# Quarter products, in-place sums and PSUM hand-over in a fused attention and SiLU kernel

## The chip, the cores and the metric

The kernel runs on one core of one Trainium2 chip. The metric is the device time of one execution in microseconds; the median of the runs is compared. All data is float32, and all work of the five engines (TensorE, VectorE, ScalarE, GpSimd, SyncE) is ordered by semaphores. In the profile they are PE (matmul) and PEld (its weight loads), DVE, ACT, POOL and SP.

## The reference, cut to what matters

```python
# q, k, v: (8, 12, 448, 64); w_in: (768, 2048); w_out: (2048, 768)
q_n, k_n = rmsnorm(q, g_q), rmsnorm(k, g_k)
attn = softmax(q_n @ k_n.T / sqrt(64))            # for each batch and head
x = (attn @ v).transpose(0, 2, 1, 3).reshape(3584, 768)
h = x @ w_in
return (h / (1 + exp(-h))) @ w_out                # (3584, 768)
```

## The kernel before

**Stages.** First comes the attention, 24 steps of four heads each (`visit`, `between`), with the product by w_in of batches that are done already mixed in between. When the last step is visited, the product by w_in of the last two batches is left; it runs alone (`halves_in` with `prepare_out` beside it). Its activated result, the 2048 features of all 3584 rows, lies in DRAM as `hidden`. The last stage is the product by w_out: seven quads of 512 rows (`quad`, L1079), each fetched from `hidden` in four pieces of 1 MB, two halves of the rows by two halves of the features.

**Seven products for eight.** Both products use the same scheme. A product of two matrices cut in 2 x 2 blocks needs eight block products; Winograd's form needs seven, and additions before and after. With a for the left side and b for the right:

```
s1 = a21 + a22   s2 = s1 - a11    s3 = a11 - a21   s4 = a12 - s2
t1 = b12 - b11   t2 = b22 - t1    t3 = b22 - b12   t4 = b21 - t2
p1 = a11 b11   p2 = a12 b21   p3 = s4 b22   p4 = a22 t4   p5 = s1 t1   p6 = s2 t2   p7 = s3 t3
u2 = p1 + p6   c11 = p1 + p2   c12 = u2 + p5 + p3
u3 = u2 + p7   c21 = u3 + p4   c22 = u3 + p5
```

The quad's left side is 512 rows by 2048 features, the right is w_out, 2048 by 768. One such product of halves is 256 rows by 1024 features by 384 columns. It can be done as one (`single`, once for each of the two tiles of 128 rows: eight multiplications with 384 columns), or by the same scheme a second time (`deep`: seven products of quarters, each of four multiplications with 192 columns). In quads 1 to 6, products 4, 7, 3 and 2 are done by seven and 1, 5 and 6 as one. In quad 0 all are done as one; beside them VectorE computes the sums of the right quarters (`sums_deep_right`) that later quads use.

**Where data lies.** The four pieces of a quad are `left[i, r]`. The quad's sums s1, s2 and s4 share one further buffer, `left_sum`; s3 overwrites a21. Sums of quarters of the features go to two alternating buffers `deep_lefts`, sums of the right quarters to `deep_rights`. All of these come by `take` from `regions`, memory of earlier stages. `stage` is one of them: it also holds the rows on their way to `hidden`.

**Who does what.** TensorE writes PSUM. ScalarE copies some products out of PSUM, VectorE adds the others to what they are added to (`plus`, L703) and makes the sums (`minus`, L700). Additions that touch no PSUM go to GpSimd where the code says `add_pool` (L1077). SyncE issues the fetches (`fetch`, L973) and the stores of results (`store`, L451), in the order of the program.

**The order.** Nothing is scheduled by a planner: within an engine, instructions run in the order in which the Python code issues them (`manual_schedule`). In `quad` the order of products is 1, 5, 4, 6, 7, 3, 2.

**PSUM.** It has eight banks. Up to the end of the w_in stage one pool, `ps`, holds them all: two `mm`, two `sc` of two banks each, `av0` and `av1`. While the w_in stage runs alone, `bank` (L725) takes these six tiles in turn, which leaves one bank of each `sc` unused. Then `banks.close()` gives the pool back, and `ps_out` opens with two banks `one` for whole products and six `seventh` for quarters. `Seven` is the w_in stage's form of the scheme; its additions `five` partly run on GpSimd.

Of the kernel before, what the change touches and what calls it, by code (L numbers as in the profile page):

```python
# [13 lines left out]
ALU = mybir.AluOpType  # L14
# [442 lines left out]
def bounded(  # L457
# [7 lines left out]
    banks = ctx.enter_context(ExitStack())  # L465
    ps = banks.enter_context(tc.tile_pool(name="ps", bufs=1, space=bass.MemoryType.PSUM))
# [255 lines left out]
    alone = False  # L722
    order = ["mm", "mm", "sc", "sc", "av0", "av1"]

    def bank(n):  # L725
        if not alone:
            return ps.tile([P, BANK], F32, name="mm", bufs=2)[:, 0:n]
        name = order[0]
        order.append(order.pop(0))
        if name == "sc":  # L730
            return ps.tile([P, 2, BANK], F32, name=name, bufs=2)[:, 0, 0:n]
        if name == "mm":
            return ps.tile([P, BANK], F32, name=name, bufs=2)[:, 0:n]
        return ps.tile([P, BANK], F32, name=name)[:, 0:n]
# [185 lines left out]
    def prepare_out(m):  # L920

        if m == HF // 2:
            for at in ((0, 0), (1, 0), (1, 1)):
                fetch(0, *at)
        for _ in range(room.CHUNK):
            rounder.open()
            yield
            rounder.round()
        if m % 2:
            right_sums(*chunk_out(ORDER[m // 2]))  # L930
        yield
# [8 lines left out]
        work, sets[1], sums_x, room.chunk(3), room.sums(3), stage, ring, parts  # L940
    ]
    regions = [[a, 0] for a in regions]

    def take(n, *which):

        for i in which:
            a, at = regions[i]
            if at + n <= a.shape[1]:
                regions[i][1] += n
                return a[:, ds(at, n)]  # L950
        raise AssertionError

    size = HF * 2 * P
    left = {(0, 0): take(size, 0), (1, 0): take(size, 0), (1, 1): take(size, 0)}
    left[0, 1] = take(size, 1)
    left_sum = take(size, 2)
    deep_lefts = [take(3 * size // 4, 3) for _ in range(2)]
    DEEP = (4, 7, 3, 2)
    deep_rights = {
        name: take(3 * 4 * QUARTER, *at).rearrange("p (s i k) -> p s i k", s=3, i=4)  # L960
        for name, at in zip(DEEP, ([4], [6], [1], [5]))
    }
    results = {at: take(2 * z.HALF, i) for at, i in (((1, 1), 0), ((2, 2), 0), ((2, 1), 6), ((1, 2), 6))}
    aside = [take(2 * z.HALF, 2) for _ in range(2)]
    copies = [[take(QUARTER, 1, 7) for _ in range(4)] for _ in range(2)]

    def fetch(q, i, r):
# [6 lines left out]

    LEFTS = {
        1: left[0, 0], 2: left[0, 1], 3: left_sum, 4: left[1, 1],
        5: left_sum, 6: left_sum, 7: left[1, 0],
    }

    def sums_left(*which):  # L980

        a11, a12, a21, a22, x = (
            a.rearrange("p (n c) -> p n c", n=2)
            for a in (left[0, 0], left[0, 1], left[1, 0], left[1, 1], left_sum)
        )
        for n in range(2):
            left_sums(
                *(a[:, n] for a in (a11, a12, a21, a22)), x[:, n], x[:, n], x[:, n], which
            )
# [5 lines left out]
    def deep_left(name):  # L995

        a = LEFTS[name].rearrange("p (i m t c) -> p m t i c", i=4, m=2, t=2)
        s = deep_lefts[DEEP.index(name) % 2].rearrange("p (s i c) -> p s i c", s=3, i=4)
        return a[:, 0, 0], a[:, 1, 0], a[:, 0, 1], a[:, 1, 1], s[:, 0], s[:, 1], s[:, 2]

    def deep_right(name, i):
        b = right_one(name, i)
        s = deep_rights[name]
        h = [ts(k, QUARTER) for k in range(2)]
        return b[:, 0, h[0]], b[:, 0, h[1]], b[:, 1, h[0]], b[:, 1, h[1]], s[:, 0, i], s[:, 1, i], s[:, 2, i]

    def sums_deep_right(name, last):

        for i in ORDER:
            b11, b12, b21, b22, t1, t2, t4 = deep_right(name, i)  # L1010
            if last:
                minus(b22, b12, b12)
            else:
                minus(b12, b11, t1)
                minus(b22, t1, t2)
                minus(b21, t2, t4)

    def of_seven(name, a, b):

        a11, a12, a21, a22, s1, s2, s4 = a  # L1020
# [3 lines left out]
            5: (s1, t1), 6: (s2, t2), 7: (a21, b12),  # L1024
        }[name]

    def deep(name, out, then=lambda t, h: None):

        a = deep_left(name)
        out = out.rearrange("p (t h k) -> p t h k", t=2, h=2)  # L1030
        p1, u2, u3, p5 = copies[DEEP.index(name) % 2]

        def product(of):
            t = ps_out.tile([P, BANK], F32, name="seventh", bufs=6)[:, 0:QUARTER]
# [4 lines left out]

        nc.scalar.copy(p1, product(1))  # L1040
        plus(product(2), p1, out[:, 0, 0])
        then(0, 0)
        plus(product(6), p1, u2)
        nc.scalar.copy(p5, product(5))
        plus(product(7), u2, u3)
        add_pool(u2, p5, u2)
        add_pool(u3, p5, out[:, 1, 1])
        plus(product(4), u3, out[:, 1, 0])
        then(1, 1)
        then(1, 0)  # L1050
        plus(product(3), u2, out[:, 0, 1])
        then(0, 1)

    def single(name, t):

        a = LEFTS[name].rearrange("p (f t c) -> p f t c", f=HF, t=2)
        o = ps_out.tile([P, BANK], F32, name="one", bufs=2)[:, 0 : z.HALF]
# [8 lines left out]
    def save_out(q, i, j, t):  # L1066
        store(
            nc, out, z, (4 * q + 2 * (i - 1) + t) * P, results[i, j][:, ts(t, z.HALF)],
            (j - 1) * z.HALF,
        )  # L1070

    def both(f):
        for t in range(2):
            f(t)

    def add_pool(a, b, o):
        nc.gpsimd.tensor_tensor(out=o, in0=a, in1=b, op=ALU.add)  # L1077

    def quad(q):  # L1079
        c = results  # L1080
        half = lambda a, t: a[:, ts(t, z.HALF)]
        which = DEEP if q > 0 else ()

        def spread(t=None):

            x, c12, c22, c21 = (
                a if t is None else half(a, t) for a in (aside[0], c[1, 2], c[2, 2], c[2, 1])
            )
            add_pool(c12, c22, c12)
            add_pool(c22, x, c22)  # L1090
            add_pool(c21, x, c21)
            for k in range(2) if t is None else (t,):
                save_out(q, 2, 2, k)
                save_out(q, 2, 1, k)

        p1 = [single(1, 0), single(1, 1)]
        fetch(q, 0, 1)
        sums_left(0, 2)
        both(lambda t: nc.scalar.copy(half(c[1, 1], t), p1[t]))
        if q == 0:  # L1100
            sums_deep_right(4, False)
        both(lambda t: nc.scalar.copy(half(c[2, 2], t), single(5, t)))
        if 4 in which:
            left_sums(*deep_left(4))
        sums_left(1)
        fetch(q + 1, 0, 0)
        if 4 in which:
            left_sums(*deep_left(7))
            deep(4, c[2, 1])
        else:  # L1110
            both(lambda t: nc.scalar.copy(half(c[2, 1], t), single(4, t)))
            sums_deep_right(7, False)
            sums_deep_right(4, True)
        fetch(q + 1, 1, 1)
        for t in range(2):
            plus(single(6, t), half(c[1, 1], t), half(c[1, 2], t))
        sums_left(3)
        if 7 in which:
            left_sums(*deep_left(3))
            deep(7, aside[0])  # L1120
            plus(aside[0], c[1, 2], aside[0])
            spread()
        else:
            for t in range(2):
                plus(single(7, t), half(c[1, 2], t), half(aside[0], t))
                spread(t)
            sums_deep_right(3, False)
            sums_deep_right(7, True)
        fetch(q + 1, 1, 0)
        if 2 in which:  # L1130
            left_sums(*deep_left(2))
        if 3 in which:
            deep(3, aside[1])
            add_pool(c[1, 2], aside[1], c[1, 2])
            both(lambda t: save_out(q, 1, 2, t))
        else:
            for t in range(2):
                plus(single(3, t), half(c[1, 2], t), half(c[1, 2], t))
                save_out(q, 1, 2, t)
            sums_deep_right(2, False)  # L1140
            sums_deep_right(3, True)
        if q == QUADS - 1:

            def last(t, h):
                columns = ds((2 * t + h) * QUARTER, QUARTER)
                rows = c[1, 1][:, columns]
                plus(rows, aside[0][:, columns], rows)
                store(
                    nc, out, z, (4 * q + t) * P, rows, h * QUARTER,
                    *((nc.scalar, nc.sync)[:: 1 if h else -1]),  # L1150
                )

            deep(2, aside[0], last)
        elif 2 in which:
            deep(2, aside[0])
            add_pool(c[1, 1], aside[0], c[1, 1])
            both(lambda t: save_out(q, 1, 1, t))
        else:
            for t in range(2):
                plus(single(2, t), half(c[1, 1], t), half(c[1, 1], t))  # L1160
                save_out(q, 1, 1, t)
        if q == 0:
# [400 lines left out]
```

## Time and profile before

| | us |
|---|---|
| median of 3 runs | 1401.07 (1399.28 to 1401.15) |
| the profiled execution | 1397.43 |
| its span in the trace | 1395.6 |
| PE busy | 1352.6 (97%) |
| DVE busy | 799.7 (57%) |
| ACT busy | 509.0 (36%) |
| POOL busy | 433.7 (31%) |
| last attention product ends, w_in alone begins | 781.0 |
| product by w_out begins | 911.3 |
| its last multiplication ends | 1389.7 |

A time in the trace is counted from the start of the span. An engine's busy time is an average over stages that have different limits; what a change in one stage is worth is read from the chain of waits in that stage. A multiplication of float32 leaves two records in the trace, so that counts of PE there are twice the number of multiplications. Tiles are named by the memory that they lie in: `work`, `x`, `sums_x`, `W`, `rows`, `stage` and `parts` in the w_out stage are the regions from which `take` cut the buffers.

### The profile page before, as it was taken

To read this page: it belongs to the slowest core of one execution; us is meant where nothing else is said; L and a number is where in the kernel's file an instruction comes from. 1 tells how busy PE (TensorE), PEld (TensorE's weight loads), DVE (VectorE), ACT (ScalarE), POOL (GpSimd) and SP (SyncE) were. 2 spreads that over 40 slices of the span, in tenths; PEclk is the share of its full clock that TensorE was granted. 3 is DMA by queue.
4 is the path that set the end of the run, shared out by engine and by line. 5 is a ranking of instruction groups with operands and counts; after the bars stand their busy time and mean duration, and the time that the engine had idled before them with its cause. 6 is when DMAs were issued, how large, how long until landed. Compare 5 with 4: busy or idle time off the path is not lost.

```text
span 1395.6 us, 18420 instructions
## 1 busy us (share of the span) xinstructions
PE 1352.6 (97%) x6849; PEld 775.0 (56%) x6849; DVE 799.7 (57%) x1157; ACT 509.0 (36%) x852; POOL 433.7 (31%) x316
## 2 busy tenths in 40 slices
PE   7998999999999999999999999989999999999998
PEld 4333444444444444444444455555687879696967
DVE  3887876765644444644444686654554545454635
ACT  6876555645455455445544254310000000000000
POOL 4664442433233333332320244401031313130403
PEclk9999999999999999999999999999999999999999
DMA  7654335333223223223211367323213232323211
GB/s 186 182 150 132 114 107 153 82 91 80 78 75 96 79 75 101 77 74 94 75 50 54 105 202 255 121 86 95 72 54 116 78 113 67 102 65 102 65 42 48
DMA packets 175686, 139.32 MB, mean 100 GB/s; under 512 B 104036, under 2 KB 159716, under 8 KB 175588
## 3 DMA queue, kind: packets, MB, share of 16 engines
q1 hardware_dynamic: 175264, 137.86, 33.2%
q8 instruction: 56, 0.92, 0.3%
q14 instruction: 42, 0.34, 0.1%
q10 hardware_dynamic: 324, 0.20, 0.0%
HBM read 88.47 MB, written 41.29 MB: 93 GB/s over the span
## 4 chain that ended last, share of the span: by engine, by line
PE 87%; DVE 6%; ACT 2%; issue 2%; DMA 1%; SPq 1%; POOL 0%; DVEq 0%; ACTq 0%; POOLq 0%
PE mm L749 26%; PE one L1060 19%; PE seventh L1037 16%; PE av L610 9%; PE sc L578 8%; PE av L749 3%; PE sc L749 3%; DVE work L653 2%; PE sc L545 1%; PE sc L560 1%; PE mm L644 1%; PE sc L644 1%; DVE rms L396 1%; DVE work L624 1%; ACT work L583 1%
## 5 line engine op out<-in xcount | busy, mean ns | idle before, releaser
L749 PE MATMUL mm<-x,W 128*128 128x448 f32 x654 | 261.0, 543 | 10.6 <-DVE stage L703 7.4
L424 POOL TENSOR_TENSOR rms<-rms,minus_half 128x14 f32<-128x14 f32 (+4 forms) x55 | 138.5, 2520 | 248.7 <-DVE rms L420 190.3
L583 ACT ACTIVATE work<-sc,rms 128x448 f32<-128x448 f32 x324 | 184.1, 631 | 86.3 <-PE sc L578 75.9
L749 PEld LDWEIGHTS mm<-x,W 128*128 128x128 f32 x654 | 121.0, 190 | 137.3 <-issue 107.8
L749 PE MATMUL mm<-sums_x,W 128*128 128x448 f32 x474 | 190.5, 542 | 2.3 <-DVE stage L703 1.5
L578 PE MATMUL sc<-work 64*64 64x448 f32 x1344 | 164.2, 546 | 5.5 <-ACT work L583 3.7
L624 DVE TENSOR_TENSOR work<-work 128x896 f32<-128x896 f32 (+1 forms) x114 | 123.3, 1115 | 76.3 <-ACT work L583 75.5
L610 PE MATMUL av<-work,rows 64*64 64x448 f32 x1296 | 153.1, 546 | 7.7 <-issue 2.9
L749 PEld LDWEIGHTS mm<-sums_x,W 128*128 128x128 f32 x474 | 88.6, 190 | 91.7 <-issue 83.0
L1060 PE MATMUL one<-W,sums_x 128*128 128x384 f32 x360 | 121.0, 486 | 0.0
L610 PEld LDWEIGHTS av<-work,rows 64*64 64x64 f32 x1296 | 51.8, 133 | 95.8 <-issue 86.1
L578 PEld LDWEIGHTS sc<-work 64*64 64x64 f32 x1344 | 51.8, 133 | 87.2 <-issue 35.4
L1060 PEld LDWEIGHTS one<-W,sums_x 128*128 128x128 f32 x360 | 68.4, 190 | 47.7
L764 POOL TENSOR_TENSOR parts<-parts,stage 128x448 f32<-128x448 f32 x31 | 42.4, 1368 | 168.3 <-DVE parts L703 168.2
L396 DVE TENSOR_REDUCE rms<-squares 112x8 f32<-112x512 f32 (+1 forms) x80 | 52.4, 655 | 63.0 <-ACT squares L395 62.1
L1060 PE MATMUL one<-W,work 128*128 128x384 f32 x216 | 72.6, 486 | 0.0
L882 ACT ACTIVATE stage<-stage 128x896 f32<-128x896 f32 x63 | 57.2, 945 | 26.2 <-DVE stage L703 25.6
L395 ACT ACTIVATE squares<-rows 128x512 f32<-128x512 f32 (+1 forms) x74 | 44.8, 605 | 57.8 <-DVE rms L396 56.7
L1040 ACT COPY x<-seventh 128x192 f32<-128x192 f32 x24 | 7.6, 318 | 156.6 <-PE seventh L1037 151.2
L1077 POOL TENSOR_TENSOR x<-x 128x192 f32<-128x192 f32 x12 | 7.1, 591 | 177.0 <-DVE x L703 177.0
L653 DVE RECIPROCAL work<-sc 128x224 f32<-128x224 f32 x36 | 55.7, 1548 | 11.1 <-PE sc L644 11.1
L700 DVE TENSOR_TENSOR sums_x<-sums_x,work 128x1024 f32<-128x1024 f32 x14 | 17.2, 1226 | 72.1 <-PE one L1060 71.7
(194 smaller groups left out, 1996.6 us busy)
## 6 DMA issues: line engine op xcount, KB each, us to landing
hidden<-stage SPq DMA_DIRECT2D x63, 448.0 KB, 2.8
work<-hidden SPq DMA_DIRECT2D x21, 1024.0 KB, 4.9
rows<-in_moe_w_out_dram SPq DMA_DIRECT2D x32, 384.0 KB, 3.2
W<-in_moe_w_in_dram SPq DMA_DIRECT2D x22, 512.0 KB, 4.6
rows<-in_k_dram SPq DMA_DIRECT2D x48, 192.0 KB, 3.0
work<-work SPq DMA_DIRECT2D x144, 56.0 KB, 1.9
rows<-in_q_dram SPq DMA_DIRECT2D x36, 224.0 KB, 3.5
x<-hidden SPq DMA_DIRECT2D x7, 1024.0 KB, 5.6
```

The source lines that it names most:

```text
L395: nc.scalar.activation(t, rows, AF.Square)
L396: nc.vector.tensor_reduce(out=out, in_=t.rearrange("p (n d) -> p n d", n=n), axis=AX.X, op=ALU.add)
L424: nc.gpsimd.tensor_tensor(out=t, in0=t, in1=half, op=ALU.pow)
L578: nc.tensor.matmul(two[ds(half * D, D), h, 0:S], keys[rows, ts(half, D)], qT[rows, pair, :], start=True, stop=True,)
L583: nc.scalar.activation(eleft[:, h] if j == LEFT else weights(c, j)[:, i, h], two[:, h, 0:S], AF.Exp, scale=norm.column(c, i, h, j),)
L610: nc.tensor.matmul(sums[i][ds(h * D, D), :], v, w, start=(j == 0 and step == 1), stop=(j == LEFT - 1 and step == 1),)
L624: nc.vector.tensor_tensor(out=total, in0=total, in1=more, op=ALU.add)
L653: nc.vector.reciprocal(out=r[0][:, rows], in_=t[:, rows])
L749: nc.tensor.matmul(t, self.left(name, s), self.right(name, s), start=s == ends[0], stop=s == ends[1])
L882: nc.scalar.activation(t, t, AF.Silu)
L1037: nc.tensor.matmul(t, x[:, i], y, start=i == ORDER[0], stop=i == ORDER[-1])
L1060: nc.tensor.matmul(o, a[:, 2 * i + m, t], right_one(name, i)[:, m], start=n == 0, stop=n == len(steps) - 1,)
```

## The change

It changes the w_out stage and the use of PSUM.

- Six of the seven products are done by seven in quads 1 to 6: 4, 2, 5, 6, 7 and 3; product 1 remains as one. In quad 0, products 7 and 3 are done by seven too. The order of products is 4, 1, 2, 5, 6, 7, 3.
- `left_sum` is gone: s1 overwrites a22, s2 overwrites a11, s4 overwrites a12 and s3 overwrites a21, as before. In the products of quarters s3 has a place of its own, and the quarters of the features are left as they are.
- Products 2, 6 and 3 are added to results that are there already (`more`), block by block, and p1 is copied twice. All additions of the stage are on VectorE, none on GpSimd. One set of `copies` takes the place of two. There are 18 buffers of right sums instead of 12 (in four larger ones).
- Of quad 0, the pieces a22, a11 and a12 are fetched during the w_in stage, a21 at the start of the quad; before, a12 was the late one.
- A pool `ps_mm` of two banks stays open for the whole kernel. The other six banks are given back when the attention is done (`others.close()`), and a pool `ps_alone` of six takes them. While the w_in stage runs alone, `bank` takes one of `ps_mm` at every fourth turn and one of `ps_alone` otherwise. In the w_out stage whole products use `ps_mm`, quarters `ps_alone`.

```diff
     def bank(n):
-        if not alone:
-            return ps.tile([P, BANK], F32, name="mm", bufs=2)[:, 0:n]
-        name = order[0]
-        order.append(order.pop(0))
...
+        turn = turns["next"] = (turns["next"] + 1) % 4
+        if ps_alone is None or turn == 0:
+            return ps_mm.tile([P, BANK], F32, name="mm")[:, 0:n]
+        return ps_alone.tile([P, BANK], F32, name="alone")[:, 0:n]
...
+    def sum_left(step):
...
+            left_sums(a11[:, n], a12[:, n], a21[:, n], a22[:, n], a22[:, n], a11[:, n], a12[:, n], (step,))
...
+    def sum_deep_left(name):
+        a11, a12, a21, a22, s1, s2, s3, s4 = deep_left(name)
+        plus(a21, a22, s1)
+        minus(s1, a11, s2)
+        minus(a11, a21, s3)
+        minus(a12, s2, s4)
...
+        def added(x, o):
+
+            if not more:
+                return x
+            plus(o, x, o)
+            return o
+
         nc.scalar.copy(p1, product(1))
-        plus(product(2), p1, out[:, 0, 0])
+        plus(product(2), added(p1, out[0][0]), out[0][0])
         then(0, 0)
         plus(product(6), p1, u2)
         nc.scalar.copy(p5, product(5))
+        plus(u2, p5, u3)
+        x = added(u3, out[0][1])
+        plus(product(3), x, out[0][1])
+        then(0, 1)
         plus(product(7), u2, u3)
-        add_pool(u2, p5, u2)
-        add_pool(u3, p5, out[:, 1, 1])
-        plus(product(4), u3, out[:, 1, 0])
-        then(1, 1)
+        x = added(u3, out[1][0])
+        plus(product(4), x, out[1][0])
+        plus(u3, added(p5, out[1][1]), out[1][1])
         then(1, 0)
-        plus(product(3), u2, out[:, 0, 1])
-        then(0, 1)
+        then(1, 1)
```

The new `quad`, without its `product` helper (which calls `deep`, or in quad 0 for products 4, 2, 5 and 6 `single` and then `sum_deep_right`) and without the last quad's stores:

```python
if q == 0:
    fetch(0, 1, 0)
    sum_deep_right(7)
product(4, c[2, 1], False)
sum_left(0)
sum_left(2)
if q == 0:
    sum_deep_right(3)
else:
    sum_deep_left(2)
for t in range(2):
    o = single(SINGLE, t)
    nc.scalar.copy(c[1, 1][t], o)
    nc.scalar.copy(c[1, 2][t], o)
sum_left(1)
if q > 0:
    sum_deep_left(5)
product(2, c[1, 1], True)
save_out(q, 1, 1)
sum_left(3)
if q > 0:
    sum_deep_left(6)
product(5, c[2, 2], False)
fetch(q + 1, 1, 1)
sum_deep_left(7)
product(6, c[1, 2], True)
fetch(q + 1, 0, 0)
sum_deep_left(3)
product(7, aside, False)
for t in range(2):
    plus(aside[t], c[1, 2][t], aside[t])
    plus(c[1, 2][t], c[2, 2][t], c[1, 2][t])
    plus(c[2, 2][t], aside[t], c[2, 2][t])
    plus(c[2, 1][t], aside[t], c[2, 1][t])
save_out(q, 2, 2)
save_out(q, 2, 1)
fetch(q + 1, 1, 0)
...
sum_deep_left(4)
product(3, c[1, 2], True)
save_out(q, 1, 2)
fetch(q + 1, 0, 1)
```

At the end of the kernel:

```diff
     visit(NC)
-    alone = True
+    others.close()
+    ps_alone = ctx.enter_context(
+        tc.tile_pool(name="ps_alone", bufs=6, space=bass.MemoryType.PSUM)
+    )
+    turns["next"] = 1
...
     run(halves_in(group, range(HF), prepare_out, begun))
-    banks.close()
-    ps_out = ctx.enter_context(tc.tile_pool(name="ps_out", bufs=1, space=bass.MemoryType.PSUM))
     for q in range(QUADS):
         quad(q)
```

## The prediction

> **What bounds the kernel now.** I read the page's chain of waits first, then the same chain in order of time over the stage that the change touches, then that stage's windows, then two pieces of timeline. The profiled execution took 1397.43 us, of which the trace spans 1395.6; the median of the runs shown is 1401.07, 3.64 above. The sums below are made against 1397.43 and their difference is then taken from the median.
>
> The page's chain, by engine and by line (the percentages are shares of the span):
>
> ```profile
> PE 87%; DVE 6%; ACT 2%; issue 2%; DMA 1%; SPq 1%; POOL 0%; DVEq 0%; ACTq 0%; POOLq 0%
> PE mm L749 26%; PE one L1060 19%; PE seventh L1037 16%; PE av L610 9%; PE sc L578 8%; PE av L749 3%; PE sc L749 3%; DVE work L653 2%; PE sc L545 1%; PE sc L560 1%; PE mm L644 1%; PE sc L644 1%; DVE rms L396 1%; DVE work L624 1%; ACT work L583 1%
> ```
>
> 35% of the span is w_out's stage: L1060 (a product as one) and L1037 (a product done by seven). The chain in order of time, one whole quad of 512 rows (start, length, what; a multiplication leaves two records):
>
> ```profile
> 1051.46 20.64 PE one L1060 x64
> 1072.10 9.10 PE seventh L1037 x56
> 1081.20 10.32 PE one L1060 x32
> 1091.52 18.20 PE seventh L1037 x112
> 1109.72 0.01 issue
> 1109.73 9.37 PE seventh L1037 x56
> 1119.10 20.64 PE one L1060 x64
> ```
>
> Two things are to be seen. A product of halves as one takes 10.32 us, by seven 9.10: 16 multiplications of 384 columns at 0.645 against 28 of 192 at 0.325. And TensorE is the path: seven products add up to 3 x 10.32 + 4 x 9.10 = 67.36 of the 67.64 us of the quad; the other 0.28 is one pause at 1109.72, where the next product waited for VectorE to empty a bank.
>
> The windows of quad 0 and of this quad (stretch, its length, busy us of PE, PEld, DVE, ACT, POOL, granted clock, DMA):
>
> ```profile
> 911.30:983.80 72.50, 72.48 (x225) 42.81 (x226) 34.62 (x75) 3.81 (x7) 6.04 (x6) 1.00 0.28 90
> 1051.50:1119.10 67.60, 67.59 (x321) 54.59 (x320) 34.41 (x47) 4.46 (x12) 15.58 (x13) 1.00 0.27 87
> ```
>
> PE is full, VectorE half idle: there is room for additions, and each TensorE microsecond taken away is a microsecond of the end.
>
> **More products by seven.** Before, quads 1 to 6 do 4 of 7 products by seven, quad 0 none. After, quads 1 to 6 do 6 (all but product 1), quad 0 does 2 (7 and 3): 2 x 6 + 2 = 14 more, each 10.32 - 9.10 = 1.22 less: **-17.1 us**. A quad becomes 10.32 + 6 x 9.10 = 64.92, quad 0 becomes 5 x 10.32 + 2 x 9.10 = 69.8. If the pause of 0.28 goes too (six quads have it): **-1.6**. It comes from the POOL additions that go (below), and p7's results no longer wait behind VectorE's slowed sums.
>
> [...] L1037 cycles through six banks already, and the granted clock in these windows is 1.00. [...] Rows give 354 to 358, so the 54 such additions of a quad cost 19.2 us[...]. That matters only if VectorE fills up:
>
> **VectorE's load, quads 1 to 6.** Sums of features, 4 steps x 2 of 1024: 8 x 1.22 = 9.8. Sums of their quarters, 6 products x 4 of 512: 24 x 0.685 = 16.4. Collecting: 7 additions of 192 for products 4, 5, 7, and 11 for 2, 6, 3, which add to an older result: 54 x 0.356 = 19.2. Final additions, 8 of 384, 0.56 each: 4.5. Together 49.9 of 64.92 us, 77%. The additions taken from POOL take 15.6 us a quad there; gone, they also stop slowing VectorE:
>
> ```profile
> 1102.07 0.68 DVE L703 TENSOR_TENSOR W<-x 128x512 f32<-128x512 f32 x1
> 1102.79 2.18 DVE L700 TENSOR_TENSOR W<-W,x 128x512 f32<-128x512 f32 x1
> 1104.89 2.29 DVE L700 TENSOR_TENSOR x<-x 128x512 f32<-128x512 f32 x1
> 1107.11 2.30 DVE L700 TENSOR_TENSOR W<-x,W 128x512 f32<-128x512 f32 x1
> ```
>
> The same sum takes 0.68 alone and 2.2 to 2.3 while POOL adds 768-wide tiles at 1102.23, 1104.50 and 1106.60 (2.1 to 2.3 each). So I use 0.685.
>
> **In-place sums: order.** s1 now overwrites a22, s2 a11, s4 a12, so each sum waits for the product that still reads the old half, and VectorE is in order behind it. Let t=0 be the start of product 4; PE then runs p4 to 9.1, p1 to 19.4, p2 28.5, p5 37.6, p6 46.7, p7 55.8, p3 64.9. VectorE: p4's last additions end at 9.9; s1 and s3 (4 x 1.22) at 14.8; quarters of a12 17.5, needed at 22 by p2's third product; s2 after p1, 21.8; quarters of s1 24.6, then p2's additions to 29.6; s4 32.0; quarters of s2 34.8, needed at 40.2. Each product's sums are ready 4 us or more early. Tightest is the seam to the next quad. From p7's end: 2 additions 0.72, 8 final ones 4.48, quarters of a22 2.74, two additions 0.71, in all 8.65 us; then the bank is empty that p4's first product takes, 9.10 after p7's end. Slack 0.45 by full durations, some 1 us more by starts (back-to-back 192s start 0.27 apart). Cost taken: 0; upper bound 1 us a seam, 6 seams.
>
> **SyncE's queue.** The fetch of the next a21 stands behind eight stores that wait for the final additions (61 us), issued at 0.5 us each, so it goes out at 65 and lands 5.1 later (the median; the longest is 10.8), at 70-71, needed at 74.8. The next a12 stands behind the stores of the last result: lands about 75, needed at 79.7. The other two have over 15 us. Cost 0.
>
> **Quad 0.** VectorE must split rights for six names, 6 x 16 additions of 192 (0.353): 33.9 us against 22.6 before, 5.65 a name. The first name's third target lies where the last hidden rows still leave for DRAM: their saves are issued from 911.18, landing 2.8 later, so VectorE, free at 911.27, stands until about 915. Then names 7 and 4 to 925, s1 and s3 930, name 3 936, s2 938.2, p2's first addition 938.8. PE, starting at 907.5, ends p2 at 938.5 and needs that bank: 0.3 lost. Later, p7's additions start at 968.2 and p3's at 977.8 where PE wants the banks at 968.5 and 977.7: 0.2 and 0.8. Total **+1.3**; bounds 0 (starts instead of durations) and 6 (saves at the longest landing seen).
>
> **PSUM handed over with the attention.** Now the old banks are given back between the two stages of products:
>
> ```profile
> 905.09 2.42 PE L749 MATMUL mm<-sums_x,W 128*128 128x448 f32 x6
> 911.32 1.56 PE L1060 MATMUL one<-x,work 128*128 128x384 f32 x4 [3.81 <-DVE stage L703]
> ```
>
> PE is done at 907.51 and waits 3.81 for the very last reader of the old banks (VectorE, 910.63 to 911.27). After, product 4 takes the two banks that stay throughout; its first was emptied long before, its second at 910.2, needed at 912.7; its features were fetched at 840, and the last sums of w_out that it reads (ready 907.71) are its last operands. **-3.8**. In exchange six banks change hands at 781.0:
>
> ```profile
> 781.24 1.15 DVE L668 TENSOR_TENSOR x<-av,work 128x448 f32<-128x448 f32 x2
> ```
>
> PE now goes straight from the last attention product to the next stage. If the new banks wait for all old readers, as at 911, it waits for this division until 782.4: **+1.4**. If only for their own address, 0. I take 1.4, since the wait at 911 was for the last of eight banks, which address alone would seldom make.
>
> **The end.** Before, two additions follow the last matmul. After, three (0.36 each), the stores on the same two queues: **+0.4**.
>
> **Sum.** -17.1 - 1.6 - 3.8 + 1.4 + 1.3 + 0.4 = -19.4. The profiled 1397.4 becomes 1378.0, the median 1401.1 becomes **1381.7**.
>
> **Rivals.** (A) Forecast as above, 1378 to 1385: chance 0.70. Its low end is no wait at 781 and none in quad 0: 1379, less 1 for scatter. (B) VectorE late: quad 0 at its bound and the seams at 1 us each, +4.7 + 6: up to 1392, about 1388 with half of it. For: VectorE at 77% with tight seams and in-order waits. Against: each quad leaves it 15 us to recover. 0.22. (C) Slower: something else slows VectorE's two-operand sums as POOL does now, say the stores and the 1 MB fetches in flight at the seam. Price: four sums at 2.2 instead of 0.685, 6.1 late, less 0.45 slack, 5.6 a seam, 34 in all: 1415. It decides from 3.7 us of lateness a seam (19.4/6 + 0.45). Against: the first sum at 1102.07 and those of quad 1052-1072 run at 0.68 with such transfers in flight. 0.03. (D) The pauses or the wait at 907 stay although the code moves (another semaphore behind them): 1385 to 1387; 0.05.
>
> A measurement of this kernel tells 0.2% (2.8 us) from no change. Only the far tail of B comes within it: same 0.02, slower 0.03, faster 0.95. The range 1376.5 to 1388 takes A, D and half of B.
>
> **What would show it.** Quads of 64.9 us with PE gapless; "one" 10.32 and "seventh" 9.10 still; VectorE near 50 us a quad and its 512-wide sums all near 0.69; PE idle under 0.3 at 907, about 1.4 at 781; short PE pauses in quad 0 released by VectorE. I am wrong if seams show PE waiting for VectorE for over 1 us, or a 512-wide sum takes over 1 us with POOL idle.

## The result

The changed kernel takes 1379.90 us (median of four runs, 1378.58 to 1381.72) against 1400.99 before: a ratio of 0.9853, 95% interval 0.9836 to 0.9870. 1381.7 was forecast. The profiled execution took 1378.58 us with a span of 1376.8, which is 18.8 less than the span before.

The page's chain of waits of the changed kernel, by engine and by line:

```profile
PE 87%; DVE 6%; ACT 3%; issue 2%; SPq 1%; DMA 1%; POOL 0%; DVEq 0%; ACTq 0%
PE mm L745 26%; PE alone L1037 25%; PE av L611 8%; PE mm L1069 8%; PE sc L579 8%; PE alone L745 7%; DVE work L654 2%; PE sc L546 1%; PE sc L561 1%; PE sc L645 1%; ACT work L584 1%; DVE work L625 1%; PE mm L645 1%; DVE rms L396 1%; DVE W L116 1%
```

The w_out stage is now L1037 with 25% (products by seven) and L1069 with 8% (as one), 33% against 35%. The chain in order of time, from product 7 of quad 0 to product 1 of quad 2 (start, length, what):

```profile
963.15 27.30 PE alone L1037 x168
990.45 10.32 PE mm L1069 x32
1000.77 54.60 PE alone L1037 x336
1055.37 10.32 PE mm L1069 x32
```

There is no line of "issue" or VectorE between them any more: a quad is 10.32 + 6 x 9.10 = 64.92 us, and TensorE goes through all seven without a pause. The windows of quad 0 and of quad 2 (stretch, length, busy us of PE, PEld, DVE, ACT, POOL, granted clock, DMA share, GB/s):

```profile
911.55:981.35 69.80, 69.80 (x274) 48.60 (x274) 55.75 (x142) 6.81 (x14) 2.22 (x2) 1.00 0.23 74
1046.27:1111.19 64.92, 64.92 (x370) 60.68 (x370) 46.31 (x95) 5.55 (x16) 0.00 (x0) 1.00 0.28 88
```

PE is busy for all of both, at full clock. VectorE has gone from 34 to 46 us a quad, GpSimd from 16 to none. The two places where PSUM changes hands, in the timeline of the changed kernel:

```profile
785.00 1.40 PE L745 MATMUL alone<-x,W 128*128 128x448 f32 x3 [1.34 <-DVE x L669]
```

and in its chain, where w_in's last product (L745) is followed by w_out's first (L1069):

```profile
909.29 2.25 PE alone L745 x6
911.55 51.60 PE mm L1069 x160
```

The wait of 3.81 us ahead of w_out is gone; one of 1.34 has come at the attention's end, released by the division. Step by step, against the two spans:

| | forecast | measured |
|---|---|---|
| 14 products by seven | -17.1 | -17.1 |
| pauses between products | -1.6 | -1.6 |
| wait ahead of w_out | -3.8 | -3.8 |
| slow start of quad 0 (72.50 for 7 x 10.32) | | -0.3 |
| wait at the attention's end | +1.4 | +1.3 |
| pauses in quad 0 | +1.3 | 0 |
| end of the kernel | +0.4 | 0 |
| attention ends later (781.0 to 783.7) | | +2.7 |
| sum | -19.4 | -18.8 |

The last row is not the change's; the runs below show whose it is.

### The profile page after: what moved, and what is told of

The parts are those of the page before. It is cut to its first block, busy times and chain, and to the rows that moved or that the text cites. A ratio compares the mean times of both kernels' runs of the same rounds, so it can differ in the third digit from the quotient of the medians.

```text
span 1376.8 us, 19392 instructions
## 1 busy us (share of the span) xinstructions
PE 1335.9 (97%) x7185; PEld 818.1 (59%) x7185; DVE 887.6 (64%) x1497; ACT 517.8 (38%) x882; POOL 338.2 (25%) x233
## 4 chain that ended last, share of the span: by engine, by line
PE 87%; DVE 6%; ACT 3%; issue 2%; SPq 1%; DMA 1%; POOL 0%; DVEq 0%; ACTq 0%
PE mm L745 26%; PE alone L1037 25%; PE av L611 8%; PE mm L1069 8%; PE sc L579 8%; PE alone L745 7%; DVE work L654 2%; PE sc L546 1%; PE sc L561 1%; PE sc L645 1%; ACT work L584 1%; DVE work L625 1%; PE mm L645 1%; DVE rms L396 1%; DVE W L116 1%
## 5 line engine op out<-in xcount | busy, mean ns | idle before, releaser
L745 PE MATMUL mm<-x,W 128*128 128x448 f32 x636 | 255.8, 546 | 10.7 <-DVE stage L704 7.4
L745 PEld LDWEIGHTS mm<-x,W 128*128 128x128 f32 x636 | 118.2, 191 | 134.1 <-issue 105.9
L745 PE MATMUL mm<-sums_x,W 128*128 128x448 f32 x456 | 183.4, 542 | 2.3 <-DVE stage L704 1.5
L745 PEld LDWEIGHTS mm<-sums_x,W 128*128 128x128 f32 x456 | 85.2, 190 | 88.4 <-issue 79.6
L1037 PE MATMUL alone<-W,rows 128*128 128x192 f32 x552 | 103.1, 326 | 0.0
L1037 PEld LDWEIGHTS alone<-W,rows 128*128 128x128 f32 x552 | 92.0, 190 | 0.0
L1069 PE MATMUL mm<-W,work 128*128 128x384 f32 x264 | 88.7, 486 | 0.0
L1037 PE MATMUL alone<-W,work 128*128 128x192 f32 x468 | 88.1, 326 | 0.0
L1037 PEld LDWEIGHTS alone<-W,work 128*128 128x128 f32 x468 | 78.1, 190 | 0.0
L1047 ACT COPY work<-alone 128x192 f32<-128x192 f32 x38 | 12.1, 319 | 165.4 <-PE alone L1037 138.1
L1069 PEld LDWEIGHTS mm<-W,work 128*128 128x128 f32 x264 | 50.2, 190 | 35.0
```

The lines of the kernel that those rows point to most:

```text
L745: nc.tensor.matmul(t, self.left(name, s), self.right(name, s), start=s == ends[0], stop=s == ends[1])
L1037: nc.tensor.matmul(t, x[:, i], y, start=i == ORDER[0], stop=i == ORDER[-1])
L1069: nc.tensor.matmul(o, a[:, 2 * i + m, t], right_one(name, i)[:, m], start=n == 0, stop=n == len(steps) - 1,)
```

## The experiments

All ratios are to the kernel before, timed on the same chip. The steps are of 1 to 4 us and the runs of one kernel lie within 2 to 7 us of each other, so the traces decide in most cases and the times only confirm.

**1. The hand-over alone.** The kernel before with the three places of the diff that concern PSUM, and with its two kinds of tiles renamed:

```diff
-        t = ps_out.tile([P, BANK], F32, name="seventh", bufs=6)[:, 0:QUARTER]
+        t = ps_alone.tile([P, BANK], F32, name="alone")[:, 0:QUARTER]
...
-        o = ps_out.tile([P, BANK], F32, name="one", bufs=2)[:, 0 : z.HALF]
+        o = ps_mm.tile([P, BANK], F32, name="mm")[:, 0 : z.HALF]
```

> The kernel before with nothing but the new use of PSUM (two banks that stay, six handed over at the end of the attention). My account: the wait of 3.8 us ahead of the first product by w_out goes, and one of 1.3 to 1.4 appears at the end of the attention, released by the division on VectorE: 2.4 to 2.5 us faster, a ratio near 0.998. Rival, that a new pool's bank waits only for whoever used the same address: no wait at the attention's end, 3.8 faster. Rival, that something else released the wait at 911 (features or sums arriving late): it stays, and the kernel is 1.4 slower.

Measured: 1397.74 us (1395.24 to 1399.43), ratio 0.9971 (0.9962 to 0.9981), which is 2.7 to 5.3 us faster; the span is 2.2 shorter. The waits of its PE from 700 us on (who waited for whom, us in total, times, longest):

```profile
PE alone L745 <- DVE x L669: 1.4, 1, 1.4
PE sc L645 <- DVE work L625: 0.3, 1, 0.3
```

The wait ahead of w_out is missing from the list, so that features or sums arriving late did not cause it. The one for the division is there. That it is a wait for the whole old pool, and not for one bank, is to be seen from the bank numbers in the programs. In this run the first product that waits takes bank 2, which held scores that ScalarE had read before, but its semaphore stands at the division's second half, which reads bank 7. In the kernel before, the first product by w_out takes bank 0, last read by VectorE at 896.32, but its semaphore stands at the read of bank 6 at 910.63. So both rivals fall. From the attention's end to the last multiplication it is 606.0 us instead of 608.6: 3.8 less, 1.4 more, and 0.27 less for a slow start of quad 0 that goes with the wait. So about 2.6 of the 19 us belong to PSUM alone and need no other part of the change; the interval of the times begins at 2.7.

**2. GpSimd's additions to VectorE alone.** The kernel before with one line changed:

```diff
     def add_pool(a, b, o):
-        nc.gpsimd.tensor_tensor(out=o, in0=a, in1=b, op=ALU.add)
+        nc.vector.tensor_tensor(out=o, in0=a, in1=b, op=ALU.add)
```

> The kernel before with GpSimd's additions of the last stage moved to VectorE, nothing else. My account: the quarter sums of 512 that took 2.2 to 2.3 us beside GpSimd take 0.68, VectorE gets to the next product's bank about 1.9 us sooner although it has more to add, and TensorE's pause of 0.28 us a quad goes: 1.6 us faster in all, and quads of 67.36. Rival, that VectorE is short of time at that seam: the three additions of 768 wide (2.9 us) in front of the sums make the pause longer, 6 quads by up to 2.9, up to 17 us slower.

Measured: 1399.31 us (1396.01 to 1402.59), ratio 0.9990 (0.9979 to 1.0001); the time alone is not clear of no change. Its chain in order of time, the end of one quad and the start of the next:

```profile
1025.56 27.30 PE seventh L1037 x168
1052.86 20.64 PE one L1060 x64
```

Three products by seven now follow each other without the 0.01 of issue and the product of 9.37 that the chain of before has in this place: the pause is gone in all six quads, a quad is 67.36. The three sums that took 2.18 to 2.30 us beside GpSimd (at 1102.79 in the kernel before) are these in the same place of a quad:

```profile
1039.54 0.69 DVE L700 TENSOR_TENSOR W<-W,x 128x512 f32<-128x512 f32 x1
1040.15 0.69 DVE L700 TENSOR_TENSOR x<-x 128x512 f32<-128x512 f32 x1
1040.75 0.69 DVE L700 TENSOR_TENSOR W<-x,W 128x512 f32<-128x512 f32 x1
```

VectorE, with more to do, has read the next product's bank 2.0 us sooner in the quad. The 1.6 us are the additions' own, and do not depend on the other parts.

**3. Two products as one again.** The changed kernel with products 5 and 6 done as one in all quads, without their quarter sums:

```diff
-            if q > 0 or name in DEEP[4:]:
+            if (q > 0 or name in DEEP[4:]) and name not in (5, 6):
```

> The changed kernel with products 5 and 6 of quads 1 to 6 done as one again, their quarter sums left out. My account, that the stage is TensorE's alone: 12 products at 10.32 instead of 9.10, 14.6 us slower, quads of 67.36 and no pause. Rival, that the seams or VectorE carry part of the time: less than 14.6, since VectorE loses 12 quarter sums and 18 additions a quad pair and pauses would close.

Measured: 1393.38 us (1392.96 to 1395.62), ratio 0.9945 (0.9926 to 0.9964). In the trace the w_out stage runs from 911.07 to 1385.04, 473.97 us, against 459.33 (911.55 to 1370.88) with both by seven: 14.64, which is the forecast 12 x 1.22. It is TensorE's stage and nothing else's.

**4. The first turn to a bank that stays.**

```diff
-    turns["next"] = 1
+    turns["next"] = 3
```

> The changed kernel with the turns begun so that the first product of w_in alone takes a bank that stays, and the second one of the six handed over. My account: the first product runs while VectorE divides, so the 1.3 us wait at the attention's end goes; 1.3 us faster, ratio 0.999. Rival, that the product waits for the division for another reason (its operand): the wait stays with the first product, no change.

Measured: 1377.65 us (1376.56 to 1380.65), ratio 0.9838 (0.9816 to 0.9861), an interval that overlaps with that of the changed kernel. In the trace w_in's first product follows the attention's last one (which ends at 783.37; the two overlap a little) with no wait, while the division runs:

```profile
783.30 2.52 PE L745 MATMUL mm<-x,W 128*128 128x448 f32 x6
783.50 1.14 DVE L669 TENSOR_TENSOR x<-av,work 128x448 f32<-128x448 f32 x2
```

The next product, at 785.66, finds its bank free. The same product with the same operands no longer waits, so the operand was not the reason; the 1.3 us were a wait for the pool that changes hands, and one number in the code avoids it.

**5 and 6. More for VectorE at the seam.** The changed kernel with one, or four, needless additions of 512 ahead of the quarter sums for the next quad:

```diff
+        sums4 = deep_left(4)
+        for _ in range(4):
+            plus(sums4[2], sums4[3], sums4[4])
         sum_deep_left(4)
         product(3, c[1, 2], True)
```

> The changed kernel with one addition of 512 wide more (done twice, same result) on VectorE at each of the six seams between quads, ahead of the quarter sums of a22. The trace of the changed kernel has VectorE empty the bank 0.94 us before TensorE wants it. If starts count (back-to-back additions of 512 start 0.61 apart), one more fits: no pause, no change. If the slack were the 0.45 that I had from whole durations, 0.2 us a seam, 1.4 us slower.

> As the last, with four additions of 512 wide more at each seam: 4 x 0.61 = 2.44 us of delay against a slack of 0.94. My account, in-order VectorE sets the seam: TensorE pauses 1.5 us at each of six seams (the first may differ), 9 us slower, and VectorE's total of 80% still leaves the rest of the quad gapless. Rival, that VectorE's mean load decides: 2.4 us more on 46 of 65 costs nothing.

Measured with one: 1378.69 us (1375.81 to 1379.81), ratio 0.9833 (0.9817 to 0.9850), and no pause in the trace. With four: 1385.80 us (1383.78 to 1386.62), ratio 0.9883 (0.9867 to 0.9900), 7 us above the run with one; the trace has this among PE's waits from 970 us on:

```profile
PE alone L1037 <- DVE work L704: 5.2, 6, 1.6
```

1.6 at the end of quad 0 and 0.72 at each of the other five seams. The list counts a pause from the end of the record before it and misses some 0.27 of each: a quad takes 65.90 us (1048.50 to 1114.40) instead of 64.92, and the stage 466.2 (909.87 to 1376.05) instead of 459.3. So 6.8 us are lost, 1.9 at the first seam and 0.98 at each of the others, which is what the times show too. VectorE is 48 us busy in 65 (1048 to 1113), so its mean load is no limit, but its place in the order at the seam is. The delay was larger and the pause smaller than I expected. The additions write the same tile and start 0.72 apart, so that four delay by 2.9; and the slack is 1.9, not 0.94. The timeline of this run at the second seam shows why:

```profile
1046.31 0.49 PE L1037 MATMUL alone<-x,work 128*128 128x192 f32 x2
1046.64 1.14 PE L1037 MATMUL alone<-W,work 128*128 128x192 f32 x6
...
1048.09 0.62 DVE L704 TENSOR_TENSOR work<-alone,work 128x192 f32<-128x192 f32 x2
1048.50 0.30 PEld L1037 LDWEIGHTS alone<-x,work 128*128 128x128 f32 x2 [1.02 <-DVE work L704]
1048.50 0.59 PE L1037 MATMUL alone<-x,work 128*128 128x192 f32 x2 [0.72 <-DVE work L704]
```

The first product of the next quad (1046.31 to 1047.78) does not wait; the second does, until VectorE has read product 2 (the first addition of 1048.09). Six banks in strict turn would have made the first one wait. The bank numbers in the program of this run explain it: the pool hands banks out in another order than in turn. At this seam product 5 of the quarters had bank 6, which ScalarE empties early, and product 2 had bank 3; the next quad's first two products take 6 and then 3. That gives VectorE one product, 1.3 us, more.

**7. The final additions on GpSimd.**

```diff
-            plus(aside[t], c[1, 2][t], aside[t])
+            add_pool(aside[t], c[1, 2][t], aside[t])
```

and likewise for the three lines that follow it.

> The changed kernel with the eight final additions of each quad on GpSimd. By what the trace of before shows, the quarter sums of a22 behind them take 2.2 us each instead of 0.68 while GpSimd adds (8 x about 1.02 us), so that VectorE, though relieved of 4.3 us, reaches TensorE's bank later than now: from 7.7 to about 9.3 us after the end of product 7, against 9.1: pauses of 0 to 1 us a seam, 0 to 6 us slower. Rival, that an idle engine helps: the sums stay at 0.68, VectorE comes 4 us sooner, no pause, no change in time.

Measured: 1380.72 us (1379.34 to 1383.36), ratio 0.9842 (0.9825 to 0.9858): no change against the changed kernel, and no pause over 0.1 us. Its timeline at a seam:

```profile
1106.06 1.48 DVE L704 TENSOR_TENSOR squares<-work 128x512 f32<-128x512 f32 x1
...
1106.95 1.44 POOL L1082 TENSOR_TENSOR x<-x,work 128x384 f32<-128x384 f32 x1
1107.58 1.37 DVE L701 TENSOR_TENSOR parts<-squares,work 128x512 f32<-128x512 f32 x1
1108.48 1.32 POOL L1082 TENSOR_TENSOR work<-work,x 128x384 f32<-128x384 f32 x1
1108.87 1.48 DVE L701 TENSOR_TENSOR rows<-work 128x512 f32<-128x512 f32 x1
```

In direction this is my account: the sums take 1.4 to 1.5 us instead of 0.68, and VectorE, relieved of eight additions, still comes 0.3 us later (product 2 is read 0.65 us ahead of the next quad's start, against 0.94). In size it is not, since 2.2 was expected of each sum; and since the true slack is 1.9 us (worked out below), nothing of it reaches the end. The rival's free help did not come either.

**8 to 10. A version that goes further.** The changed kernel with the turns of run 4 and product 6 of quad 0 by seven too:

```diff
-            if q > 0 or name in DEEP[4:]:
+            if q > 0 or name in DEEP[3:]:
...
         product(2, c[1, 1], True)
+        if q == 0:
+            sum_deep_right(6)
```

The right sums of 2 follow ahead of product 6 of quad 0, those of 5 in quad 1 ahead of the quarter sums of s1.

> The changed kernel with the turns of the fourth run, and product 6 of quad 0 done by seven too: its right sums are made after product 2 instead of those of 2, which follow ahead of product 6, and those of 5 move to quad 1. My account: 1.22 us less in quad 0 and 1.3 at the attention's end, 2.5 us faster, if VectorE keeps up; VectorE's work is the same plus one set of quarter sums. Rival: VectorE is late in quad 0 or 1 and TensorE pauses there by as much.

> The changed kernel as it is, for a comparison with the next run on the same chip and for the scatter of the attention: its code there is the same as in the other variants, so if the 2.66 us by which the attention ended later than before come from the change, it ends near 783.7 again; if they come from the granted clock of the first 250 us, it ends between 781 and 787, later by about half of the extra time at half clock. The w_out stage takes 459.3 us either way.

> The version with product 6 of quad 0 by seven and the other order of turns, beside the changed kernel on the same chip. From the traces: 1.22 less in quad 0 and 1.3 less at the attention's end, 2.5 us faster, a ratio between the two of 0.998. Rival: the gains lie within scatter and the two come out the same.

Measured, run 8: 1376.62 us (1375.56 to 1377.42), ratio 0.9815 (0.9799 to 0.9832). Runs 9 and 10, side by side: the changed kernel 1377.78 (1376.46 to 1378.84), ratio 0.9829 (0.9815 to 0.9843); this version 1376.40 (1375.64 to 1378.44), ratio 0.9821 (0.9807 to 0.9834). In the traces quad 0 takes 68.58 us instead of 69.80, no product waits for VectorE, and the wait at the attention's end is gone; the times, 1.4 apart, do not separate the two. That it is 2.5 us faster is read from the trace alone.

Run 9 also settles the table's last row. Its attention ends at 781.45, not 783.66, with the same code, so the delay is not the change's. What differs is the granted clock: from 0 to 250 us it is 0.99 in run 9 and 0.98 in the changed kernel's first profile. The windows from 100 to 140 us of the changed kernel's first profile (the clock is the number after the POOL column):

```profile
100.00:140.00 40.00, 35.59 (x268) 14.06 (x264) 29.34 (x41) 24.95 (x44) 19.86 (x10) 0.96 0.44 112
```

and of the kernel before:

```profile
100.00:140.00 40.00, 34.55 (x274) 13.78 (x276) 30.64 (x44) 25.55 (x45) 20.39 (x11) 1.00 0.47 123
```

Over the twelve profiles, by the time that the trace's record of the clock has at half speed in the first 250 us:

| at half speed, us | attention ends at, us | profiles |
|---|---|---|
| 3.4 | 781.0 to 782.0 | before, 1, 5, 6, 9 |
| 6.8 | 782.7 to 783.4 | 2, 3, 4 |
| 10.2 | 783.7 to 784.5 | after, 8, 10 |
| 13.7 | 786.4 | 7 |

The end moves with the time at half speed, by about half of it, whichever the kernel.

## Why the prediction was right

**TensorE is the path, and a product by seven is worth 1.22 us.** Right to 0.1 us; run 3 takes it back by itself, 14.64 us for twelve products.

**The pauses go with GpSimd's additions.** Right, and run 2 shows that they, not the new order, do it: with the old order and without GpSimd's additions a quad takes 67.36 us instead of 67.64.

**PSUM.** Both waits came out as forecast, and run 1 has them without the rest. That a new pool's first bank waited for the last reader of the whole old pool was argued from one wait; the wait at the division, whose banks are two of six, is the second case of it, and the bank numbers given under run 1 show that in neither case it was the new tile's own bank.

**VectorE's load and the seam.** The load was forecast at 49.9 us a quad; the window has 46.3. Two terms were off. I had summed whole rows, but independent additions start before the one ahead of them has ended, as the changed kernel's seam shows (one sum of 512 and the two additions into the second bank):

```profile
1108.24 0.68 DVE L701 TENSOR_TENSOR rows<-work 128x512 f32<-128x512 f32 x1
1108.85 0.68 DVE L701 TENSOR_TENSOR rows<-work,parts 128x512 f32<-128x512 f32 x1
1109.45 0.35 DVE L704 TENSOR_TENSOR work<-work 128x192 f32<-128x192 f32 x1
1109.90 0.62 DVE L704 TENSOR_TENSOR work<-alone,work 128x192 f32<-128x192 f32 x2
...
1112.16 0.35 PEld L1037 LDWEIGHTS alone<-x,work 128*128 128x128 f32 x2
```

Rows of 0.68 start 0.61 apart, and two of 192 take 0.62 together. By 1110.25 product 2's bank is read, 0.94 us ahead of the next quad (1111.19), not 0.45. And it is the next quad's second product that takes this bank; its weights begin to load at 1112.16, the last line above. The slack at this seam is therefore 1.9 us. At the end of quad 0 it is 1.0 (981.30 to 982.32), where the sums of the right quarters for product 6 (964.66 to 968.5) have made VectorE late. Run 6 agrees with both: 2.9 us of delay cost 0.98 and 1.9. The forecast of no pause held, but its account of which product takes the bank was wrong.

**Quad 0's +1.3 did not come.** This is the term that was mis-sized. The mechanism is there: VectorE stood for the last hidden rows, 3.15 us, as this row of the changed kernel's timeline shows, and was then late:

```profile
919.38 0.36 DVE L701 TENSOR_TENSOR stage<-x,W 128x192 f32<-128x192 f32 x1 [3.15 <-DMA hidden<-stage]
...
939.66 0.55 DVE L704 TENSOR_TENSOR parts<-mm,parts 128x384 f32<-128x384 f32 x1
```

But the 16 additions of one name took 4.8 us (932.59 to 937.39), where 16 whole rows of 0.353 made 5.65. Over three names that is 2.5 us, so product 2's bank was being emptied from 939.66 on, well ahead of product 2's end at 942.5 (911.55 + 3 x 10.32). That was the lower bound that the forecast gave for this term. The two pauses later in quad 0 did not come either: product 7's first additions start at 971.06 and product 3's at 980.94, 1.2 and 0.9 us sooner against TensorE than forecast (its start is 4.05 us later here than the 907.5 of the forecast).

**The end's +0.4.** From the last multiplication to the end of the span it is 5.9 us in both: three additions take 0.25 longer than two, and the span does not end later by it.

**What no step had.** The attention's 2.7 us go with the clock, which differs between executions of the same code (0.98 and 0.99 from 0 to 250 us in the two profiles of the changed kernel). That the traces' sum came within 0.6 us of the forecast is in part luck: these 2.7 us stand against 1.7 of pauses and end that did not come and 0.3 of a slow start that nobody had counted. With the attention of run 9 the span is 1374.7, 20.9 less than before; the steps without that row make 21.5. The median's 21.1 lies between.

**The rivals.** Runs 5 and 6 give the slower one its measure: with 2.9 us of added lateness a seam 6.8 us were lost in all, and by an estimate from the slacks of 1.9 and 1.0 the point from which it would have decided lies at about 5 us a seam (19.4 / 6 + 1.75), not 3.7. Run 7 makes the seam's sums slow in the way that this rival supposed, though to 1.4 to 1.5 us and not to 2.2, and loses nothing. That the stores or fetches at the seam slow VectorE is not seen: the sums of 512 there take 0.68 to 0.69.

## What to carry to other kernels

Where one engine is gapless for a whole stage, as TensorE is here, the value of a change is that engine's time, to a tenth of a microsecond (14.64 us measured in run 3 for 12 x 1.22), and every other engine only has to be in time; what "in time" means is set by the bank that the stage's engine wants next, so find that bank before counting slack. Count a chain of independent vector additions by the distance of their starts, not by the length of their rows (0.61 us against 0.68 for those of 512 here), and a chain that hands results on by no less than the full rows (0.72 from start to start in the changed kernel, at 1106.91 and 1107.63, where s2 reads s1). When a memory pool is closed and another opened, look for the wait at the border (3.81 and 1.34 us here), and let the first work behind it use memory that did not change hands.

## What the runs showed of the hardware that was not expected

GpSimd's price for VectorE depended on GpSimd's instruction, not only on VectorE's. The same 512-wide sum of two SBUF operands took 0.68 us alone, 1.4 to 1.5 beside GpSimd additions of 384 (run 7; 0.99 to 1.00 each at 1102.78 to 1104.92, ahead of those sums), and 2.2 to 2.3 beside those of 768 (the kernel before; 1.81 at 1044.13, beside one VectorE row of 0.36). In both cases the rows of the two engines start by turns, one of VectorE for one of GpSimd. In the kernel before, VectorE's sums start at 1102.79, 1104.89 and 1107.11 and GpSimd's additions at 1102.23, 1104.50 and 1106.60; in run 7 it is 1107.58, 1108.87 and 1110.28 against 1106.95, 1108.48 and 1109.88. What makes them do so was not tried.

TensorE's granted clock fell to half for 3.4 us or twice that early in the span: for 3.41 from 18.49 us on in the kernel before, for 6.83 from 17.42 on in the changed kernel's first profile; from 0 to 40 us it was 0.91 or 0.96 in these two and in runs 1 to 8. From 100 to 140 us it was 0.91 to 0.96 in the changed kernel's first profile and in runs 2, 4, 7 and 8, and 1.00 in the kernel before and in runs 1, 3, 5 and 6, although the code up to there is the same in runs 3 to 8. Near 109 us TensorE waits for VectorE: 2.73 us in the changed kernel's first profile, where the clock fell at 109.58, and 2.76 in the kernel before, where it did not. A wait of the same kind near 240 us, 2.61 in the kernel before and 2.64 in the changed one, stands at a clock of 1.00 in both. The end of the attention has so moved by up to 5 us (781.0 to 786.4 in the table above), and a profile's span with it; what decides whether the clock falls was not tried.
